# Two attention blocks on one core: loads in one fixed order instead of a simulated queue's order

## Chip, core and metric

The kernel runs on one core of one Trainium2 chip. The metric is the device time of one execution in microseconds (us), median of several. "Span" is the profiled execution from its first to its last instruction, some 2 us less than the device time of that execution. Ratios are the mean time of one kernel's fast runs over the mean of the kernel before's fast runs in the same rounds on the same chip, so they are not quite the ratio of the medians quoted.

## The reference

Twice (A and B, with their own inputs), and concatenated at the end:

```python
B, Sq, D = 16, 64, 640;  H, Sk, Dh = 32, 512, 128          # all bfloat16
q = (x @ wq).reshape(B, Sq, H, Dh).transpose(0, 2, 1, 3)
scores = einsum("bhqd,bhkd->bhqk", q, k_cache) * Dh ** -0.5
p = softmax(scores, axis=-1)
o = einsum("bhqk,bhkd->bhqd", p, v_cache)
out = o.transpose(0, 2, 1, 3).reshape(B, Sq, H * Dh) @ wo
```

The K and V caches are 268 MB of the 292 MB that have to be read.

## The kernel before

The work is cut into 128 *packs*: pack n has four heads of two batches, with two K loads, two V loads (512 KB each), score products, softmax, PV products and a share of the output product. A pack's steps stand at fixed fractions of a "slot" (`AT`), pipelined over some five slots. K has a ring of six packs (`NK`), V of four (`NV`). There are four phases of 32 packs; each has its own wq and wo weights. Loads are listed with a desired time, a time from which their buffer is free, and a rank; a simulated DMA queue puts them in order:

```python
AT = dict(..., KT=(-1.24, -1.0), S=0, ..., PV=1.75, OE=(2.0, 2.06), ..., OP=2.31, ...)
DMA_US = dict(LDK=1.27, LDV=1.29, LDWQ=1.5, LDWO=1.75, LDX=0.45)
# V of pack n (called for n = -2 and -1 too: packs that only fill the pipeline)
op = add("sp", "LDV", (n, b), tv - 0.3, [], [("v", n % cfg.NV, b)])
ready = n - cfg.NV + AT["PV"] + 0.2 if n >= cfg.NV - 2 else -99.0
loads.append((tv - 0.05 if n >= 0 else -99.0, ready, 3, op))
# K of pack n
ready = n - cfg.NK + AT["KT"][b] + 0.25 if n >= cfg.NK else -99.0
loads.append((tk - 0.05, ready, 2, op))
...
add("dve", "VZ", 0, -9.9, [], [("v", i % cfg.NV, b) for i in (-2, -1) for b in range(2)])   # memset of two V slots
add("dve", "BZ", 0, -9.8, ...); add("dve", "WZ", 0, -9.7, ...)                                # two more memsets
...
pending = sorted(loads, key=lambda e: (e[0], e[2])); t_now = -7.0
while pending:
    cand = [e for e in pending[:64] if e[1] <= t_now]        # free buffers first, by desired time
    ...
    progs["sp"].append(e[3])
```

SyncE ("SP") then issues that list in order. Before each load it waits for whoever used the buffer last; the list of such waits comes from the resource names (`("v", slot, b)`). A V load of pack -2 or -1 moves nothing: it is a placeholder that waits like a load and then only raises the semaphore.

```python
if n < 0:
    return None, None            # em_LDV
...
for s, v in waits:
    e.wait_ge(sem[s], v * units(s))
first, last = emitters[kind](e, op)
if last is None:
    e.sem_inc(sem[op.sem], units(op.sem))
    return
```

Of the kernel before, what the change touches and what calls it, by code (L numbers as in the profile page):

```python
# [17 lines left out]
class Cfg:  # L18
# [7 lines left out]
    NR = 2  # L26
    PERIOD = 4
    BASE = 32
    WIDE = (0, 1, 2)
    SLOT_US = 5.6  # L30
    AT = dict(XT=-2.485, XE=-2.28, XC=-0.9, QP=-0.45, QE=-0.24, KT=(-1.24, -1.0), S=0,
              EX=(0.21, 0.32, 0.43, 0.54), RC=(0.53, 0.75), NM=(0.56, 0.69, 0.82, 0.95), TR=1.2,
              TE=(1.26, 1.39), PV=1.75, OE=(2.0, 2.06), ZO=2.11, OP=2.31, OS=2.53, ST=3.374, WP0=-1.75, WP1=-1.6)
    DMA_US = dict(LDK=1.27, LDV=1.29, LDWQ=1.5, LDWO=1.75, LDX=0.45)


class Op:
# [19 lines left out]
def build_plan(dims, cfg, general):  # L57
# [4 lines left out]
    NPH, NBP, NJ = dims["NPH"], dims["NBP"], dims["NJ"]  # L62
    PH = NBP * NJ
    N = NPH * PH
    AT = cfg.AT
    ops = []
    loads = []
    at = {}

    def add(eng, kind, idx, ts, reads=(), writes=()):  # L70
        op = Op(eng, kind, idx, ts, reads, writes)
        ops.append(op)
        at[(kind, idx)] = op
        return op

    def add_output(n):
        g, j = n // NJ, n % NJ
        final = n >= 0 and dims["FINAL"](g // NBP)
        for b in range(2):
            tv = n + AT["PV"]  # L80
            op = add("sp", "LDV", (n, b), tv - 0.3, [], [("v", n % cfg.NV, b)])
            ready = n - cfg.NV + AT["PV"] + 0.2 if n >= cfg.NV - 2 else -99.0
            loads.append((tv - 0.05 if n >= 0 else -99.0, ready, 3, op))
        if n > -2:
            add("pe", "TR", n, n + AT["TR"], [("pn", i) for i in range(4)] + [("ident",)], [("B", 4), ("B", 5)])
        for b in range(2):
            add("dve", "TE", (n, b), n + AT["TE"][b], [], [("B", 4 + b), ("pT", b)])
        add("pe", "PV", n, n + AT["PV"], [("pT", 0), ("pT", 1), ("v", n % cfg.NV, 0), ("v", n % cfg.NV, 1)],
            [("B", 4), ("B", 5), ("B67",)])
        add("act", "OE", (n, 1), n + AT["OE"][0], [], [("B67",), ("oT", 1)])  # L90
        add("act", "OE", (n, 0), n + AT["OE"][1], [], [("B", 4), ("B", 5), ("oT", 0)])
        add("act", "ZO", n, n + AT["ZO"], [("zeros",)], [("B67",)])
        add("pe", "OP", n, n + AT["OP"], [("oT", 0), ("oT", 1), ("wo", j)], [("B67",)])
        if j == NJ - 1:
            bp = g % NBP
            add("dve", "OS", g, n + AT["OS"], [("acc", bp)], [("B67",), ("out_sb",) if final else ("acc", bp)])
            if final:
                add("act", "ST", g, n + AT["ST"], [("out_sb",)], [("out_dram", g)])
# [4 lines left out]
    for g in range(N // NJ + 1):  # L103
        n0 = g * NJ
        txt = n0 + AT["XT"]
        add("pe", "XT", g, txt, [("xn", g % cfg.NXN), ("ident",)], [("SB", 0)])
        if g == N // NJ:
            break
        if dims["FIRST"](g // NBP):
            add("act", "XE", g, n0 + AT["XE"], [], [("SB", 0), ("xs", g % NBP)])  # L110
            op = add("sp", "LDX", g, txt - 0.5, [], [("xn", g % cfg.NXN)])
            loads.append((txt - 2.4, (g - cfg.NXN) * NJ + AT["XT"] if g > cfg.NXN else -7.0, 0, op))
        add("pool", "XC", g, n0 + AT["XC"], [("xs", g % NBP)], [("xT", g % cfg.NX)])
    for ph in range(NPH):
        twp = [ph * PH + j + (AT["WP1"] if ph else AT["WP0"]) for j in range(NJ)]
        for kt in range(dims["KT"] if ph else 0):
            ready = twp[-1] - PH + 0.5 if ph > 1 else NJ - 1 + AT["WP0"] + 0.5
            op = add("sp", "LDWQ", (ph, kt), twp[0] - 0.5, [], [("ws", kt, j) for j in range(NJ)])
            loads.append((ready + 0.5 + 0.5 * kt if ph == 1 else ready + 2.0 + 0.14 * PH * kt, ready, 1, op))
        for j in range(NJ):  # L120
            w = ph * NJ + j
            n0 = ph * PH + j
            add("pool", "WP", w, twp[j], [("ws", kt, j) for kt in range(dims["KT"])], [("wqp", j)])
            if not ph:
                op = add("sp", "LDWQ", (0, j), twp[j] - 0.5, [], [("ws", kt, j) for kt in range(dims["KT"])])
                loads.append((twp[j] - 0.3, -99.0, 1, op))
            tuse = n0 + AT["OE"][0]
            op = add("sp", "LDWO", w, n0 + AT["OP"] - 0.8 * NJ, [], [("wo", j)])
            ready = n0 - NJ + AT["OP"] + 0.2 if ph else -99.0
            loads.append((tuse - 0.3, ready, 4, op))  # L130
    if not general:
        add("pool", "PZ", 0, -9.95, [], [("zeros",)])
    add("dve", "VZ", 0, -9.9, [], [("v", i % cfg.NV, b) for i in (-2, -1) for b in range(2)])
# [3 lines left out]
    for n in range(-2, N):  # L137
        add_output(n)
        if n < 0:
            continue  # L140
        g, j = n // NJ, n % NJ
        add("pe", "QP", n, n + AT["QP"], [("xT", g % cfg.NX), ("wqp", j)], [("SB", 1)])
        add("act", "QE", n, n + AT["QE"], [], [("SB", 1), ("qs", n % cfg.NQ)])
        for b in range(2):
            tk = n + AT["KT"][b]
            add("dve", "KT", (n, b), tk, [("kn", n % cfg.NK, b)], [("kt", n % cfg.NKT, b)])
            op = add("sp", "LDK", (n, b), tk - 0.9, [], [("kn", n % cfg.NK, b)])
            ready = n - cfg.NK + AT["KT"][b] + 0.25 if n >= cfg.NK else -99.0
            loads.append((tk - 0.05, ready, 2, op))
        add("pe", "S", n, n + AT["S"], [("qs", n % cfg.NQ), ("kt", n % cfg.NKT, 0), ("kt", n % cfg.NKT, 1)],  # L150
            [("SB", i) for i in range(4)])
        for i in range(4):
            h = 4 * n + i
            te = n + AT["EX"][i]
            if general:
                add("dve", "MX", h, te - 0.002, [], [("SB", i), ("negmax", h % 4)])
            add("act", "EX", h, te, [("negmax", h % 4)] if general else [],
                [("SB", i), ("p", h % cfg.NP), ("rs", h)])
            add("pool", "NM", h, n + AT["NM"][i], [("p", h % cfg.NP), ("recip", n % cfg.NR, i // 3)], [("pn", i)])
        for a in range(2):  # L160
            add("dve", "RC", (n, a), n + AT["RC"][a], [("rs", 4 * n + i) for i in ((0, 1, 2), (3,))[a]],
                [("recip", n % cfg.NR, a)])
# [3 lines left out]
        add("dve", "FLC", 0, N - 1 + AT["TE"][1] + 0.002, [], [("SB", 0), ("flag",)])  # L166

    progs = {e: sorted((o for o in ops if o.eng == e), key=lambda o: o.ts) for e in ENGINES if e != "sp"}
    progs["sp"] = []
    pending = sorted(loads, key=lambda e: (e[0], e[2]))  # L170
    t_now = -7.0
    while pending:
        cand = [e for e in pending[:64] if e[1] <= t_now]
        if cand:
            e = cand[0]
        else:
            e = min(pending[:64], key=lambda e_: (e_[1], e_[0], e_[2]))
            t_now = float(e[1])
        pending.remove(e)
        progs["sp"].append(e[3])  # L180
        if e[3].kind != "LDV" or e[3].idx[0] >= 0:
            t_now += cfg.DMA_US[e[3].kind] / cfg.SLOT_US

    last_writer = {}
    readers = {}
# [87 lines left out]

    base = {("q_" + eng,): cfg.BASE for eng in ("act", "dve", "pool")}
    counts = dict(base)
# [163 lines left out]
def mha_kernel(nc, blocks, out, cfg=None):  # L439
# [13 lines left out]
    NH = NBLK * NBP * H  # L453
    WIDE = cfg.WIDE

    plans = []
    for general in (False, True):
        dims = dict(NPH=NPH, NBP=NBP, NJ=NJ, KT=KT, FIRST=lambda ph: ph % NSUB == 0,
                    FINAL=lambda ph: ph % NSUB == NSUB - 1)
        plans.append(build_plan(dims, cfg, general))  # L460
    NK, NV, NKT, NX, NXN, NQ, NP, NR = (cfg.NK, cfg.NV, cfg.NKT, cfg.NX, cfg.NXN, cfg.NQ, cfg.NP, cfg.NR)

    with contextlib.ExitStack() as es:
# [101 lines left out]
        def em_LDV(e, op):  # L565
# [5 lines left out]
            dst = v_ring[:, n % NV, b]  # L571
            if j in WIDE:
                ins = e.dma_start(dst.rearrange("p t d -> p (t d)"), src.rearrange("h (p t) d -> (h p) (t d)", t=16))  # L573
# [73 lines left out]
        def exp_views(h):  # L647
            src, dst = ps[:, h % 4, :], p_ring[:, h % NP, :]
            if h // 4 % NJ in WIDE:
                return src, dst  # L650
# [22 lines left out]
        def em_NM(e, op):  # L673
            h = op.idx
            i = h % 4
            if h < 0:
                ins = e.memset(pn_sb[:, :, :].rearrange("p t c -> p (t c)"), 0.0)
                return ins, ins
            if h // 4 % NJ in WIDE:
                dst = pn_sb[:, :, 32 * i:32 * i + 32]  # L680
# [29 lines left out]
        def em_PV(e, op):  # L710
            n = op.idx
            wide = n % NJ in WIDE
            tall, tiles, per = (32, 4, 16) if wide else (64, 2, 8)
# [93 lines left out]
        def run_program(e, eng, p):  # L807
# [7 lines left out]
            for key in sorted(counts):  # L815
                if key[0].startswith("q_"):
                    e.sem_inc(sems[p][key], cfg.BASE)
            for op in prog[:lo]:
# [100 lines left out]
```

## Time and profile before

| | before |
|---|---|
| device time, median of 3 | 766.59 us |
| span of the profiled execution | 764.1 us |
| loaded from HBM | 292.03 MB |
| PE / DVE / ACT / POOL busy | 89 / 69 / 68 / 53 % |
| last V lands | 744.1 us |

The last row is from the trace's landing records: each load raises its semaphore in 16 steps, and the sixteenth is the landing (the two V loads of a pack share a semaphore, so a V landing here is the second one's). PE's busy share counts pipelined products, so by the profile page's own legend it is not the share of its peak. One more view is SyncE's own waits (who waited, for whom; us in all, times, longest us):

```profile
SPq L562 <- PE ps L636: 43.2, 26, 3.3
SPq L573 <- PE ps L721: 24.8, 19, 4.1
...
SPq L800 <- DVE v_ring L525: 4.5, 1, 4.5
```

Line 562 issues K, line 573 V; line 800 is the placeholder's semaphore increment.

### The profile page before, as it was taken

The page shows a single profiled execution, that of the slowest core. Times are in us where ns is not written, and L with a number is a line of the kernel's source. Part 1 is how long each engine was busy: PE and PEld are TensorE (multiplying, and loading weights), DVE is VectorE, ACT ScalarE, POOL GpSimd, SP SyncE. Part 2 cuts the span into 40 slices and gives each one's busy share as a digit, 9 for nine tenths or more (in the row PEclk, how much of TensorE's full clock was granted, in tenths as well). Part 3 has the DMA queues.
Part 4 walks back from the last instruction along what each step waited for, and adds up shares of the span by engine and source line. Part 5 has one row for each costly group of instructions (what it writes and reads, how often), then busy time and mean ns, then how long its engine had stood idle before and what let it go on. Part 6 is the DMA issues. An engine that isn't in the chain of part 4 may idle for free.

```text
span 764.1 us, 57362 instructions
## 1 busy us (share of the span) xinstructions
PE 681.7 (89%) x26518; PEld 527.6 (69%) x26518; DVE 529.5 (69%) x814; ACT 518.8 (68%) x1559; POOL 406.7 (53%) x584
## 2 busy tenths in 40 slices
PE   1659999999999899998988889999999899899995
PEld 1437777777777677776766667777777677777773
DVE  6527777777777767776776677776776576677772
ACT  1437777778777767766766767777766577667773
POOL 4515554554875445554585445555477455454542
PEclk9979999999999999999999999999999999999999
DMA  6999999999999999999999999999999999999960
GB/s 221 390 398 405 408 405 406 405 406 406 407 395 404 407 406 407 407 408 409 406 401 394 405 406 408 405 406 404 406 407 394 397 407 408 407 408 408 406 255 15
DMA packets 99806, 295.15 MB, mean 386 GB/s; under 512 B 9264, under 2 KB 24112, under 8 KB 99760
## 3 DMA queue, kind: packets, MB, share of 16 engines
q1 hardware_dynamic: 97456, 292.06, 97.8%
q10 hardware_dynamic: 2304, 2.62, 1.0%
q14 instruction: 36, 0.29, 0.1%
q8 instruction: 10, 0.16, 0.1%
HBM read 292.03 MB, written 2.62 MB: 386 GB/s over the span
## 4 chain that ended last, share of the span: by engine, by line
SPq 38%; PE 28%; DMA 18%; POOL 6%; issue 5%; DVE 4%; ACT 0%; POOLq 0%; DVEq 0%; ACTq 0%
SPq L562 16%; SPq L573 11%; DMA v_ring<-in_B_v_cache_dram 8%; PE ps L721 7%; SPq L575 6%; PE ps L741 6%; PE ps L636 6%; PE ps L613 5%; POOL pn_sb L686 5%; DMA v_ring<-in_A_v_cache_dram 4%; PE ps L697 4%; DMA kn_ring<-in_A_k_cache_dram 3%; DVE pT_sb L707 2%; SPq L539 2%; DMA kn_ring<-in_B_k_cache_dram 2%
## 5 line engine op out<-in xcount | busy, mean ns | idle before, releaser
L686 POOL TENSOR_SCALAR pn_sb<-p_ring,recip 128x512 bf16<-128x512 bf16 x512 | 344.5, 692 | 330.0 <-DVE recip L670 330.0
L626 DVE STREAM_TRANSPOSE kt_ring<-kn_ring 128x1024 f32<-128x1024 f32 x256 | 307.3, 1225 | 62.2 <-DMA kn_ring<-in_B_k_cache_dram 34.7
L657 ACT ACTIVATE p_ring<-ps 128x512 bf16<-128x512 f32 x512 | 298.3, 598 | 26.4 <-PE ps L636 21.2
L707 DVE COPY pT_sb<-ps 128x1024 bf16<-128x1024 bf16 x258 | 165.3, 682 | 128.9 <-PE ps L697 128.8
L721 PE MATMUL ps<-pT_sb,v_ring 32*128 32x64 bf16 (+1 forms) x14528 | 156.1, 192 | 34.0 <-DMA v_ring<-in_B_v_cache_dram 9.8
L721 PEld LDWEIGHTS ps<-pT_sb,v_ring 32*128 32x128 bf16 (+1 forms) x14528 | 141.7, 92 | 49.1 <-DMA v_ring<-in_B_v_cache_dram 16.2
L741 PE MATMUL ps<-wo_sb,oT_sb 128*128 128x320 bf16 x1040 | 166.0, 303 | 6.0 <-issue 5.0
L613 PE MATMUL ps<-xT_ring,wqp_sb 128*128 128x128 bf16 x2560 | 165.4, 220 | 5.6 <-POOL xT_ring L602 5.6
L729 ACT ACTIVATE oT_sb<-ps 128x256 bf16<-128x256 f32 x260 | 85.6, 381 | 122.5 <-PE ps L721 108.3
L613 PEld LDWEIGHTS ps<-xT_ring,wqp_sb 128*128 128x128 bf16 x2560 | 157.1, 114 | 11.9 <-issue 5.9
L636 PE MATMUL ps<-kt_ring,qs_ring 32*64 32x512 bf16 x4096 | 147.9, 399 | 0.0
L619 ACT ACTIVATE qs_ring<-ps 128x512 bf16<-128x512 f32 x128 | 76.4, 597 | 81.1 <-PE ps L613 80.8
L697 PEld LDWEIGHTS ps<-ident,pn_sb 64*128 64x128 bf16 x4128 | 70.4, 95 | 83.6 <-ACT ps L733 53.5
L741 PEld LDWEIGHTS ps<-wo_sb,oT_sb 128*128 128x128 bf16 x1040 | 91.7, 98 | 43.8 <-issue 5.5
L657 ACT ACTIVATION_READ_ACCUMULATOR p_ring<-ps 128x1 f32 x512 | 106.7, 208 | 0.0
L697 PE MATMUL ps<-ident,pn_sb 64*128 64x64 bf16 x4128 | 84.0, 191 | 23.1 <-POOL pn_sb L686 14.0
L636 PEld LDWEIGHTS ps<-kt_ring,qs_ring 32*64 32x64 bf16 x4096 | 55.9, 104 | 31.7 <-issue 1.4
L670 DVE RECIPROCAL recip<-rowsum 128x3 f32<-128x3 f32 (+1 forms) x256 | 37.6, 161 | 32.2 <-ACT p_ring L657 28.0
L733 ACT ACTIVATE ps<-zeros 128x256 f32<-128x256 bf16 x130 | 51.5, 396 | 0.0
L585 POOL COPY wqp_sb<-ws_sb 128x1280 bf16<-128x1280 bf16 x32 | 39.2, 1254 | 11.9 <-DMA ws_sb<-in_A_wq_dram 11.9
L602 POOL COPY xT_ring<-xs_sb 128x640 bf16<-128x640 bf16 x32 | 22.9, 716 | 3.1 <-PE ps L613 3.1
L592 PE MATMUL ps<-ident,xn_ring 128*128 128x128 bf16 x165 | 14.8, 222 | 8.0 <-DMA xn_ring<-in_A_x_dram 8.0
(25 smaller groups left out, 65.3 us busy)
## 6 DMA issues: line engine op xcount, KB each, us to landing
kn_ring<-in_A_k_cache_dram SPq DMA_DIRECT2D x128, 512.0 KB, 13.7
v_ring<-in_A_v_cache_dram SPq DMA_DIRECT2D x128, 512.0 KB, 13.5
kn_ring<-in_B_k_cache_dram SPq DMA_DIRECT2D x128, 512.0 KB, 14.7
v_ring<-in_B_v_cache_dram SPq DMA_DIRECT2D x128, 512.0 KB, 12.1
wo_sb<-in_A_wo_dram SPq DMA_DIRECT2D x8, 640.0 KB, 13.1
ws_sb<-in_B_wq_dram SPq DMA_DIRECT2D x10, 512.0 KB, 13.5
wo_sb<-in_B_wo_dram SPq DMA_DIRECT2D x8, 640.0 KB, 13.4
ws_sb<-in_A_wq_dram SPq DMA_DIRECT2D x4, 640.0 KB, 9.1
```

The lines of the kernel that those rows point to most:

```text
L562: ins = e.dma_start(kn_ring[:, n % NK, b, :], src)
L573: ins = e.dma_start(dst.rearrange("p t d -> p (t d)"), src.rearrange("h (p t) d -> (h p) (t d)", t=16))
L613: last = e.matmul(ps[:, 1, f * 128:(f + 1) * 128], w[:, kt, f, :], xT_ring[:, xs, kt, :], start=(kt == 0), stop=(kt == KT - 1))
L626: ins = e.transpose(dst, kn_ring[:, n % NK, b, :].bitcast(F32))
L636: last = e.matmul(ps[64 * b:64 * b + 64, i, :], qs_ring[rows, n % NQ, f, b, :], kt_ring[rows, n % NKT, b, :, f // 2, :, f % 2], start=(f = ...
L657: ins = e.activation(dst, src, ACTF.Exp, scale=1.0, accum_out=rowsum[:, h:h + 1])
L686: ins = e.tensor_scalar(dst, src, recip[:, h // 4 % NR, i:i + 1], 1.0, ALU.mult, ALU.mult)
L697: last = e.transpose(pt_bank(b)[:, 64 * c:64 * c + 64], pn_sb[rows, c, :], ident[rows, rows], tile_position=(64 * b, 0))
L707: ins = e.tensor_copy(pT_sb[:, b].rearrange("p t q -> p (t q)"), pt_bank(b))
L721: last = e.matmul(ps[:, 4 + i, 64 * b:64 * b + 64], v_ring[rows, n % NV, b, c, :], pT_sb[rows, b, c, :], start=(t == 0 and i < 2), stop=(t ...
L729: ins = e.activation(oT_sb[:, 2 * a:2 * a + 2, :], o_ps[:, 2 * a:2 * a + 2, :], ACTF.Copy)
L741: last = e.matmul(out_ps[:, s, :], oT_sb[:, i, :], wo_sb[:, 4 * j + i, s * NH0:(s + 1) * NH0], start=(j == 0 and i == 0), stop=(j == NJ - ...
```

## The change

Its intent: drop the simulated queue and give every load a fixed time in slots: V when its slot comes free, K so that it stands beside the V of three packs earlier, x and weights early. The core of the diff:

```diff
+    KLEAD = 2.5
-            op = add("sp", "LDV", (n, b), tv - 0.3, [], [("v", n % cfg.NV, b)])
-            ready = n - cfg.NV + AT["PV"] + 0.2 if n >= cfg.NV - 2 else -99.0
-            loads.append((tv - 0.05 if n >= 0 else -99.0, ready, 3, op))
+            op = add("sp", "LDV", (n, b), tv - 0.3, [], [("v" if n >= 0 else "absent", n % cfg.NV, b)])
+            loads.append((n - cfg.NV + AT["PV"] + 0.2 if n >= 0 else -99.0, 3, op))
 ...
-            ready = n - cfg.NK + AT["KT"][b] + 0.25 if n >= cfg.NK else -99.0
-            loads.append((tk - 0.05, ready, 2, op))
+            loads.append((n - cfg.NV + AT["PV"] + 0.2 - cfg.KLEAD, 2, op))
 ...                                   (x, wq and wo loads: their times alike)
-    pending = sorted(loads, key=lambda e: (e[0], e[2]))
-    t_now = -7.0
-    while pending: ...
+    progs["sp"] = [e[2] for e in sorted(loads, key=lambda e: e[:2])]
```

## The prediction

> **What bounds the kernel now.** I read the page's slices first, then a table by stretches, then the waits of single stretches, then the chain that ended last, and last the trace's landing records.
>
> The page: DMA share by slice, GB/s by slice, and the queue that carries all loads.
>
> ```profile
> DMA  6999999999999999999999999999999999999960
> GB/s 221 390 398 405 408 405 406 405 406 406 407 395 404 407 406 407 407 408 409 406 401 394 405 406 408 405 406 404 406 407 394 397 407 408 407 408 408 406 255 15
> q1 hardware_dynamic: 97456, 292.06, 97.8%
> ```
>
> All slices but the first and the last two move 390 to 409 GB/s. 292.06 MB at 406 GB/s take 719 us of the 764.1 us span: the load stream is nearly the whole kernel. A K or V load is 512 KB, so 0.524 MB / 406 GB/s = 1.29 us; a pack (2 K, 2 V) is 5.2 us. The order of issue sets only *which* load is late, and what is left to do when the last has landed.
>
> Stretches (us, PE, PEld, DVE, ACT, POOL busy, PE clock, DMA share, GB/s):
>
> ```profile
> 100.00:200.00 100.00, 98.38 (x3884) 76.84 (x3883) 75.96 (x119) 77.52 (x233) 54.56 (x81) 1.00 1.03 406
> 600.00:700.00 100.00, 92.78 (x3638) 71.48 (x3634) 71.63 (x109) 68.99 (x210) 50.25 (x75) 0.98 1.03 408
> 735.00:740.00 5.00, 4.96 (x174) 3.77 (x165) 4.22 (x8) 3.66 (x12) 1.91 (x3) 1.00 0.69 248
> 740.00:745.00 5.00, 4.66 (x191) 3.60 (x176) 3.13 (x6) 3.66 (x12) 2.71 (x5) 1.00 0.15 57
> ```
>
> From 60 to 207 us PE is the bound (98% busy; no wait for a load in that stretch) although DMA is saturated too. Later PE is at 91 to 93% and waits for loads, until about 707 us. After 730 us DMA runs out of work and PE is the bound again. The waits between 600 and 710 us that a DMA ended:
>
> ```profile
> PEld ps L721 <- DMA v_ring<-in_B_v_cache_dram: 7.7, 9, 2.0
> PE ps L721 <- DMA v_ring<-in_B_v_cache_dram: 5.0, 6, 1.6
> DVE kt_ring L626 <- DMA kn_ring<-in_B_k_cache_dram: 4.3, 2, 3.8
> ACT oT_sb L729 <- DMA wo_sb<-in_B_wo_dram: 2.1, 1, 2.1
> ```
>
> Late in the kernel it is V that is late, in many small waits (PE pauses before the PV product, L721); K only twice. The chain from its last DMA on:
>
> ```profile
> 691.07 16.75 DMA v_ring<-in_B_v_cache_dram
> 707.81 0.05 issue
> 707.86 1.22 PE ps L721 x128
> 709.07 1.06 PE ps L636 x23
> ```
>
> The PV product at 707.86 us is pack 118's (counted back from pack 127's, at 754.98). From there to the end, 56 us, the chain holds no DMA: PE, POOL and DVE set the pace. That pace, from starts of PV products where nothing is late:
>
> ```profile
> 70.24 1.22 PE L721 MATMUL ps<-pT_sb,v_ring 32*128 32x64 bf16 x128
> ...
> 75.67 1.22 PE L721 MATMUL ps<-pT_sb,v_ring 32*128 32x64 bf16 x128
> ...
> 91.33 1.22 PE L721 MATMUL ps<-pT_sb,v_ring 32*128 32x64 bf16 x128
> ```
>
> 70.24 to 91.33 is four packs: 21.09 us, 5.27 a pack. The stream needs 5.2 plus weights and x. The two are level, which is why a small shift in the order can decide who waits.
>
> **What the Trainium skill says.** "DMA: Bandwidth & Descriptors", section Queues, rings and completion order: each DMA engine consumes a ring's descriptors in ring order. So the order in which SyncE issues is the order in which loads come. The trace agrees: by the landing records, consecutive loads finish about 1.28 us apart in the issued order. The same page, Specifications, gives a fabric ceiling of 435 GB/s; the trace's 406 is below it, and nothing in the change alters sizes or packets, so I expect no other rate. "Trace Analysis", section DMA Instruction — HWDGE: the recorded issue holds neither the semaphore wait nor the data movement, so I take a load's lateness from landings and from the waits of PE and DVE, not from issue durations.
>
> **The change part by part.** Instructions on PE, ACT, DVE and POOL stay the same, in the same order (comparing both built programs); so do the 563 loads and all ring depths. Only SyncE's sequence moves.
>
> 1. *K's lead.* Before, SyncE's order came from a simulated queue, which sent K as far ahead as six K slots allow. The waits of the DMA queue show it: loads of K waited 43.2 us in 26 waits for the score product that frees a K slot. Late in the kernel the order is V118, K123, V119, K124 ...; after, it is V118, K121, V119, K122. So pack 118's V stood before 28 loads (10 K, 18 V) and now stands before 32 (14 K, 18 V). The stream ends at the same moment, so V118 lands 4 x 1.28 = 5.1 us earlier, 702.7 instead of 707.8 us. From 92 to 123 all V move by 0 to 4 loads in this way. That is the gain: V was on the path, K lay ready about 8 us (K121 landed at 699.1).
>
> 2. *What takes V's place.* K121 now lands two loads behind V118, at 705.2 us. DVE transposes it in two halves of 1.23 us, and these stand before the PSUM copies that the next PV needs. Between packs 68 and 91 the kernel before had just this order (V68, K71 ...), and the landing records show K there 1.8 to 2.5 us after the PV product's start at the cost of 0 to 0.6 us a pack. So K costs about 0.5 us of the 5.1: 4.6 left.
>
> 3. *PE's own pace as a cap.* After the last weights (the wo load of pack 99) nothing but K and V comes. PV of pack 101 started at 613.94 us. If nothing were late after it: 24 packs x 5.27 = 126.5 to pack 125 (740.4), plus the 19.0 us that lay between pack 125's PV (745.10) and the end: 759.4, which is 4.7 us less than 764.1. Parts 1 and 3 agree, so about 4.6 us is all there is.
>
> 4. *Weights.* The wo load of a pack now stands after both halves of a K, one load later than before (V97, K100, K100, wo 13). ACT's copy (L729) will wait up to 3 us instead of up to 2.6 at eight places. But the same bytes precede V100 in both orders, and DMA bounds there. 0 to 0.3 us lost, in my estimate. wq of phase 1 is spread among packs 4 to 7 instead of five in a row at 48 us; at that time PE is slowed by pauses labelled "issue", so nothing is gained.
>
> 5. *V issued as soon as its slot is free, K behind it.* SyncE now stops at each V until PV of four packs earlier is done. Nothing runs dry: at 71 us V8 is issued 9.7 us before its first piece lands, with the same loads ahead of it in both orders. While PE is the bound (60 to 207 us) that margin shrinks by 5.27 - 5.19 = 0.08 us a pack, 2 us over 24 packs. 0 us.
>
> Sum: -5.1 + 0.5 + 0.2 = about -4.4 us of 764. The measured time is 766.59, so 762.2.
>
> **Rivals.** *(a) SyncE's stops starve the queue.* For it: each V now waits, and K is stuck behind it with its slot free. Against: the 9.7 us of queue at 71 us, and later landings 13 to 18 us after issue. If it happened from 60 to 207 us, DMA share would fall below 1.0 there, and each percent of 147 us costs 1.5 us; the time would be 766 to 772. *(b) K becomes the bound.* K's lead over V's shrinks from about 8 us early to 2.5 us behind V's landing; if DVE's order makes each late K cost the full 2.5 us, the gain is halved: 764. Against: packs 68 to 91 ran that way. *(c) The end is DMA's anyway.* V127 landed at 744.1, and its PV started 10.9 us later, so that slack takes the whole shift; a gain above 10 us is impossible because the same stream ends at 744.1 in any order without gaps. *(d) The head gains.* V2 and V3 come four loads earlier, wq later; PE started its real pace at 59 us because of pauses that no load ended. DMA's saturation after it swallows it: 0.
>
> **Range and chances.** Centre 762.2: part 3's cap gives 761.9, rival (b) 764, a few pauses more 765. Below 759 a second mechanism would be needed. Range 759.0 to 765.5. Two per cent is 15.3 us: faster by that would need the stream itself to be shorter (2%), slower would need starvation over most of the run (3%).
>
> **What would show it.** Right: DMA share stays 1.03 from 60 to 730 us; the K loads' waits for score products (L562's) vanish and SyncE waits at V; waits of PE at L721 for V after 600 us fall from 12.7 us (both rows) to under 4, waits of DVE for K rise; the last load still lands at 743 to 745 us while PE ends near 759.5; the gap from last landing to the end falls from 20 to about 16 us. Wrong if: DMA share dips in the first 200 us (a), DVE's waits for K reach tens of us late on (b), or the stream ends at another time.

## The result and the profile after

The changed kernel takes 758.43 us (757.98 to 759.13, 4 runs) against 766.69 us (4 runs) in the same rounds: ratio 0.9894, 95% interval 0.9876 to 0.9911. That is 8.1 us by the ratio, nearly twice the 4.4 us predicted, and below the range of 759.0 to 765.5. The span is 756.0 us.

The page's DMA share and GB/s by slice:

```profile
DMA  8999999999999999999999999999999999999980
GB/s 309 394 398 405 406 407 407 405 405 406 403 395 406 406 408 406 407 407 408 408 399 395 406 407 408 405 405 405 406 406 397 394 408 407 407 408 407 406 326 20
```

The middle is as before. The first slice has 309 GB/s instead of 221: at 18.9 us a slice that is 5.8 MB against 4.2 MB, 1.6 MB more, or 4 us of the stream. The load stream *starts earlier*. The head of the timeline says by how much (start us, us, what); before:

```profile
1.71 3.47 DVE L525 MEMSET v_ring<- 128x4096 uint32 x1 [1.71 <-PEq L904]
5.48 0.40 SPq L539 DMA_DIRECT2D xn_ring<-in_A_x_dram  x1
```

and after:

```profile
1.04 0.40 SPq L521 DMA_DIRECT2D xn_ring<-in_A_x_dram  x1
1.49 0.42 SPq L531 DMA_DIRECT2D ws_sb<-in_A_wq_dram  x1
1.71 3.47 DVE L507 MEMSET v_ring<- 128x4096 uint32 x1 [1.71 <-PEq L886]
```

Before, the first load went out 0.30 us after the V ring's memset ended at 5.18 us; after, it goes out at 1.04 us, while that memset has not begun. SyncE's waits after:

```profile
SPq L555 <- PE ps L703: 78.0, 38, 6.0
SPq L557 <- PE ps L703: 26.8, 9, 4.2
```

The 4.5 us row for the memset is gone. So are K's waits; SyncE now stops at V, as intended. The cause is one word of the diff: placeholders now write the resource `"absent"` instead of `"v"`, so they no longer depend on the memset. They stand first in SyncE's list, so before, the whole list stood behind them.

The same stretches as in the prediction (PE, PEld, DVE, ACT, POOL busy, PE clock, DMA share, GB/s), then the waits of 600 to 710 us that a DMA ended, then the last DMA on the chain that ended last:

```profile
100.00:200.00 100.00, 98.37 (x3885) 76.94 (x3885) 76.18 (x120) 77.21 (x232) 55.92 (x83) 1.00 1.03 406
600.00:700.00 100.00, 97.14 (x3779) 75.70 (x3780) 74.07 (x116) 74.08 (x226) 51.75 (x77) 0.98 1.03 407
735.00:740.00 5.00, 4.99 (x220) 4.02 (x220) 1.53 (x4) 3.64 (x12) 2.69 (x4) 1.00 0.18 68
```

```profile
ACT oT_sb L711 <- DMA wo_sb<-in_B_wo_dram: 3.3, 1, 3.3
```

```profile
587.88 12.35 DMA wo_sb<-in_B_wo_dram
600.23 0.02 issue
600.25 0.67 ACT oT_sb L711 x2
```

From 600 to 700 us PE rises from 93 to 97% busy, and no wait for V or K is left; the one DMA wait is ACT's, for the last wo load (wo 15, of pack 99). From 600.2 us to the end the chain holds no DMA. Before, that point was at 707.8 us.

So there are two candidates: the start (4.4 us earlier) and the order late in the kernel. The trace alone doesn't say how they add up. In particular the prediction had argued that an early start is swallowed.

### The profile page after: what moved, and what is told of

Read it like the earlier page. It is cut to its first block, busy times and chain, and to the rows that moved or that the text cites. A ratio compares the mean times of both kernels' runs of the same rounds, so it can differ in the third digit from the quotient of the medians.

```text
span 756.0 us, 57362 instructions
## 1 busy us (share of the span) xinstructions
PE 685.2 (91%) x26518; PEld 530.0 (70%) x26518; DVE 533.2 (71%) x814; ACT 518.5 (69%) x1559; POOL 406.7 (54%) x584
## 4 chain that ended last, share of the span: by engine, by line
PE 40%; SPq 20%; DMA 17%; POOL 9%; DVE 8%; issue 4%; ACT 1%; POOLq 0%; DVEq 0%; ACTq 0%
PE ps L723 10%; PE ps L703 9%; POOL pn_sb L668 9%; PE ps L595 8%; SPq L544 8%; PE ps L618 7%; SPq L555 6%; PE ps L679 6%; DMA kn_ring<-in_B_k_cache_dram 6%; DMA kn_ring<-in_A_k_cache_dram 5%; SPq L557 4%; DMA wo_sb<-in_B_wo_dram 3%; DVE pT_sb L689 3%; DMA v_ring<-in_B_v_cache_dram 2%; DVE kt_ring L608 1%
## 5 line engine op out<-in xcount | busy, mean ns | idle before, releaser
L723 PE MATMUL ps<-wo_sb,oT_sb 128*128 128x320 bf16 x1040 | 169.7, 307 | 6.9 <-issue 5.9
```

Source lines behind the costliest of these rows:

```text
L723: last = e.matmul(out_ps[:, s, :], oT_sb[:, i, :], wo_sb[:, 4 * j + i, s * NH0:(s + 1) * NH0], start=(j == 0 and i == 0), stop=(j == NJ - ...
```

## The experiments

All were timed with five rounds. "x us by the ratio" is (ratio difference) x 766.7.

| run | median us | ratio to before, 95% interval |
|---|---|---|
| changed kernel | 758.43 | 0.9894 (0.9876 to 0.9911) |
| order_only | 763.47 | 0.9947 (0.9932 to 0.9962) |
| start_only | 762.33 | 0.9942 (0.9928 to 0.9957) |
| late_inc | 761.61 | 0.9934 (0.9914 to 0.9954) |
| vz_last | 771.54 | 1.0055 (1.004 to 1.0069) |
| tail_only | 761.91 | 0.9944 (0.9931 to 0.9958) |
| head_only | 766.50 | 0.9999 (0.9986 to 1.0013) |
| lead_4_5 | 764.47 | 0.9976 (0.9962 to 0.999) |
| lead_1_5 | 760.12 | 0.992 (0.9907 to 0.9934) |
| wo_early | 757.63 | 0.9891 (0.9876 to 0.9905) |
| less_wq3 | 752.85 | 0.9831 (0.9818 to 0.9845) |
| less_v | 758.94 | 0.9905 (0.9888 to 0.9921) |
| tail_early | 757.08 | 0.9879 (0.9864 to 0.9895) |

### Which part makes the gain?

*order_only*: the changed kernel with the dependency put back.

```diff
-[("v" if n >= 0 else "absent", n % cfg.NV, b)])
+[("v", n % cfg.NV, b)])
```

> The changed kernel with one part undone: the two placeholder V loads of packs -2 and -1 again wait for DVE's memset of the V ring, so the first load is issued at about 5.5 us instead of 1.0 us. Theory A (the gain has two parts that add: loads start 4.4 us earlier, and the new order of K and V): 762.2 to 762.9 us, that is the changed kernel's 758.4 plus 3.8 to 4.5, and the last V lands at 744 us as in the kernel before. Rival B (the early start is swallowed because DMA is saturated afterwards anyway, and the order is worth the whole 8 us): 758.4 to 759. Rival C (the start alone makes the gain, the order is worth nothing): 766.7.

*start_only*: the kernel before with `"absent"` alone (the same line, the other way).

> The kernel before with that one part alone: the placeholders no longer wait for the memset; order of loads as before. Theory A: 762.3 to 763.0 us, the last V lands 3.7 to 4.4 us earlier than 744.1, waits for V late in the kernel as in the kernel before. Rival B: 766.7. Rival C: 758.4.

The order alone is worth 0.0053, 4.1 us; the start alone 0.0058, 4.4 us. Together 8.5, measured 8.1: they add. Theories B and C fall. In the profiled runs start_only's first load goes out at 1.04 us and its last V lands at 739.8 us (before: 744.1), and its waits for V between 600 and 710 us are 7.5 us (PEld) and 3.8 us (PE), before 7.7 and 5.0: the whole stream has moved 4.3 us, and V is about as late within it as before.

### Is it really the wait at the head of SyncE's list?

*late_inc* keeps the dependency and moves only the placeholders' place in the list of the kernel before:

```diff
+    absent = [o for o in progs["sp"] if o.kind == "LDV" and o.idx[0] < 0]
+    progs["sp"] = [o for o in progs["sp"] if o not in absent]
+    progs["sp"][8:8] = absent
```

> The kernel before; the wait for the memset is kept, but the placeholders stand after the first eight loads in SyncE's order instead of ahead of the first. If what costs is that the wait stands at the head of SyncE's line (theory A): as start_only within 0.5 us, first issue at about 1.0 us. If the missing dependency itself did something else: 766.7.

It gives 0.9934, within its interval the same as start_only; its first load goes out at 0.79 us. So the dependency did no harm there; its place at the head of the list cost the time.

*vz_last* makes the wait longer without adding work: the memset comes third on DVE instead of first.

```diff
-    add("dve", "VZ", 0, -9.9, ...)
+    add("dve", "VZ", 0, -9.6, ...)
```

> The kernel before with DVE's three memsets in another order: the V ring's comes last, so it ends about 4.4 us later (1.76 us for the PSUM memset and 2.19 us for the wo memset go ahead of it, with gaps), and nothing is added. Theory A: the first load is issued at about 9.9 us and the end moves by the same: 770.6 to 771.4 us. Rival B (saturation swallows the start): 766.7 to 767.5.

Its head (start us, us, what):

```profile
3.58 2.19 DVE L533 MEMSET wo_sb<- 128x2560 uint32 x1 [0.52 <-issue]
6.57 3.47 DVE L525 MEMSET v_ring<- 128x4096 uint32 x1 [0.80 <-issue]
10.34 0.40 SPq L539 DMA_DIRECT2D xn_ring<-in_A_x_dram  x1
```

The first load goes out 4.9 us later than before (10.34 against 5.48) and the kernel takes 0.0055, 4.2 us longer. From 1.0 to 5.5 to 10.3 us of first issue the time goes up by 4.4 and 4.2 us: almost one for one.

### Where does the order pay?

*tail_only* is the kernel before (its early wait kept) with its own order up to the V of pack 100 and the changed kernel's order from there; *head_only* is the mirror. `fixed` holds the changed kernel's times.

```diff
+    cut = fixed[id(at[("LDV", (100, 1))])]
+    key = lambda o: fixed[id(o)]
+    progs["sp"] = ([o for o in progs["sp"] if key(o) <= cut]
+                   + sorted((o for o in progs["sp"] if key(o) > cut), key=key))
```

> The kernel before (wait for the memset kept): its own order up to the V of pack 100, and from there on the changed kernel's order. Theory A2 (the order pays only through V of the last quarter; earlier order is swallowed because the same bytes have to come): 761.5 to 763 us, as order_only (763.5) or up to 1.5 us less, since the wo loads of packs 96 to 99 keep their old place. Rival (the whole order has to change): 766 to 767.

> The mirror of tail_only: the changed kernel's order up to the V of pack 100, then the order of the kernel before; the wait for the memset kept. If the order pays only after pack 100: 766 to 767.5, as the kernel before. If the earlier order pays too: 764 to 765.

tail_only has the whole of it (0.0056, 4.3 us), head_only nothing (0.0001). Both predicted values were met. Up to pack 100 another order of the same bytes changed nothing; after it, 28 packs of order were worth 4 us.

The trace of tail_only shows something that the changed kernel hides. Between 600 and 710 us:

```profile
DVE kt_ring L638 <- DMA kn_ring<-in_B_k_cache_dram: 15.6, 25, 3.9
```

In the changed kernel no such row is left there. In tail_only the wo loads keep their old, earlier places. Pack 101's PV product starts at 613.8 us (in order_only at 615.7), and the K loads land 1.3 to 2.1 us after the start of the PV product of three packs earlier; in the changed kernel it is 0.3 us before to 0.6 us after (packs 100 to 124, every third one read). The last DMA on the chain of tail_only is a K load that landed at 732 us. So which load is the last to be needed differs between these two kernels, though their order after pack 100 is the same.

### How much lead of K is right?

*lead_4_5* and *lead_1_5* are the changed kernel with another lead from pack 9 on:

```diff
-            loads.append((n - cfg.NV + AT["PV"] + 0.2 - cfg.KLEAD, 2, op))
+            loads.append((n - cfg.NV + AT["PV"] + 0.2 - (4.5 if n > 8 else cfg.KLEAD), 2, op))
```

> The changed kernel with K's lead at 4.5 packs instead of 2.5 from pack 9 on (K of pack n+5 behind V of pack n, as the kernel before has it near its end). Theory A2: every late V stands behind four more loads, 5.1 us; in the changed kernel V lay ready 2.0 to 2.8 us before its product from pack 104 on, so 2.3 to 4 us are lost: 760.7 to 762.5, and PE waits for V again after 600 us. Rival (K's lead is not what pays, the fixed order is): 758.4.

> The changed kernel with K's lead at 1.5 packs from pack 9 on: K of pack n+2 behind V of pack n, so K comes two loads (2.56 us) later against its use. In the changed kernel K lands between 0.7 us before and 0.6 us after the PV product's start from pack 100 on, and up to 2 us after it cost nothing. So DVE's waits for K rise and the time with them, by 0.5 to 2 us: 759 to 760.5. If K has more room than I think: 758.4 or less.

lead_4_5 loses 0.0082, 6.3 us: more than expected, and not as expected. PE waits for no V after 600 us. The last DMA on its chain is wo 15:

```profile
594.11 12.11 DMA wo_sb<-in_B_wo_dram
```

It landed at 606.2 us, where the changed kernel's landed at 600.2. Four more K loads (5.1 us) stand ahead of it, and they pass to the end in full; I had reckoned with a V that had 2 to 2.8 us to spare. The other 0.9 us of the 6.0 I have not traced.

lead_1_5 loses 0.0026, 2.0 us, at the upper end of what was expected (the two intervals just overlap), and the expected wait is in its trace. Between 600 and 710 us, and the last DMA on its chain up to 710 us:

```profile
DVE kt_ring L608 <- DMA kn_ring<-in_B_k_cache_dram: 15.4, 24, 3.8
```

```profile
694.13 14.05 DMA kn_ring<-in_B_k_cache_dram
```

In the changed kernel neither is there in that stretch: K two loads later has to be waited for by DVE. The sum of the row does not measure the loss, though: tail_early below has a like one (16.9 us in 25 waits, 580 to 710 us) and is not slower than the changed kernel. So 2.5 lies between a lead that delays what else is needed and one that delays K itself.

### What bounds the changed kernel?

*wo_early* puts each wo load ahead of the two K loads before it (`AT["OP"] + 0.2` becomes `AT["OP"] + 0.1`).

> The changed kernel with the wo load of a pack issued right behind V of the same j, ahead of the two K loads behind which it stands now. In the changed kernel the last load on the chain is wo 15 (ACT waits 3.3 us for it, 6.9 us in three waits between 580 and 620 us) and from there the chain holds no load. Two loads less ahead of it are 2.56 us, K of packs 99 to 102 come 1.6 us later. Theory (wo bounds, then PE's pace to the end): 1 to 2.5 us less, 756 to 757.4. If K takes wo's place: 758 to 759.

It gains 0.0003: a miss. Between 580 and 620 us its waits are

```profile
DVE kt_ring L608 <- DMA kn_ring<-in_B_k_cache_dram: 10.4, 4, 3.8
PEld ps L703 <- DMA v_ring<-in_B_v_cache_dram: 5.4, 3, 2.0
ACT oT_sb L711 <- DMA wo_sb<-in_B_wo_dram: 5.2, 2, 3.0
```

In the changed kernel they were 1.7 us for K, none for V and 6.9 us for wo. A K load took wo's place: the last DMA on the chain of wo_early is a K that landed at 600.4 us, where wo 15 of the changed kernel landed at 600.2. At pack 100 the kernel has asked for everything loaded so far. Two runs that are wrong test that.

*less_wq3* takes bytes away *before* pack 100 (packs 69 to 90), *less_v* takes three times as many away *after* it:

```diff
-                ins = e.dma_start(ws_sb[:, i].rearrange("p j c -> p (j c)"), src[:, i, c:c + NJ * 512])
+                few = 1 if ph == 3 else NJ
+                ins = e.dma_start(ws_sb[:, i, 0:few].rearrange("p j c -> p (j c)"), src[:, i, c:c + few * 512])
```

```diff
-            if j in WIDE:
+            if n >= 108 and b == 1 and j in WIDE:
+                ins = e.dma_start(dst[:, 0:4, :].rearrange("p t d -> p (t d)"),
+                                  src.rearrange("h (p t) d -> (h p) (t d)", t=16)[:, 0:4 * DH])
+            elif j in WIDE:
```

> The changed kernel, made wrong on purpose: the five wq loads of the last phase (issued between packs 69 and 90) bring a quarter of their bytes, 1.97 MB less in all, 4.8 us at 406 GB/s. If the load stream bounds up to pack 100 (theory): 4 to 5 us less, 753.4 to 754.4. If PE or something else bounds there: under 1 us less.

> The changed kernel, made wrong on purpose: 15 V loads of packs 108 to 126 bring a quarter of their bytes, 5.9 MB less in all, 14.5 us at 406 GB/s. If from pack 101 on PE's own pace sets the end (theory): 0 to 1 us less, 757.4 to 758.4. If the load stream still bounds at the end: 5 us less or more.

1.97 MB less before pack 100: 0.0063, 4.8 us less than the changed kernel, the size of its 4.8 us of stream. 5.9 MB less after pack 100: no gain (0.9905 against 0.9894, intervals overlap), although the last V now landed at 733.7 instead of 740.5 us. So the changed kernel is one piece after the other: the load stream sets the time up to pack 100, PE's pace from there. less_v takes bytes only from pack 108 on; for packs 101 to 107 the evidence is the chain, which holds no DMA after 600.2 us. (less_wq3 passed the comparison with the reference although it used stale wq columns. The reference's inputs explain that, as an estimate from reference.py: q is about 0.01 and K 0.1 in size, so the scores are about 0.001 and the softmax is almost even, whatever wq is.)

### A version that beats both?

*tail_early* joins the best parts: order of the kernel before up to pack 100, the changed one after it, no wait for the memset.

> tail_only with the early start: the order of the kernel before up to pack 100 (wo loads one or two loads earlier than in the changed kernel), the changed kernel's order after it, and no wait for the memset. The two parts add: 761.9 - 4.4 = 757.5; it beats the changed kernel only if the wo waits (3.3 us at wo 15) cost it something: 756.5 to 758.

757.08 us, 0.9879: clearly better than the kernel before. Against the changed kernel (0.9894) the intervals overlap; 1 us may be there, the runs don't settle it.

## Why the prediction was wrong, point by point

- **The step that failed** is the premise under the change part by part, "Only SyncE's sequence moves", with part 1's "The stream ends at the same moment", rival (c)'s "the same stream ends at 744.1 in any order without gaps", and rival (d)'s "DMA's saturation after it swallows it: 0". The change also took away a wait: 4.4 us (start_only). The stream begins 4.4 us earlier, and its last V landed at 740.5 us, not 744.1. The 0.9 us that this lacks of 4.4 goes with the new order: the last V of start_only landed the full 4.3 us earlier, that of order_only 1.4 us later than before (745.4 us). The 4.5 us row stood in SyncE's waits of the kernel before and the word `"absent"` in the diff. I read both and joined neither to the other.
- Rival (d) had the logic upside down. If a saturated stream bounds the time, *order* at its head is swallowed (head_only: nothing), but its *start* is not: every later byte moves with it (start_only, late_inc, vz_last).
- **Part 1, K's lead:** right in size. The order alone gave 4.1 us where the sum said 4.4, all of it after pack 100 (tail_only). V118 landed at 703.5 us in order_only, where the prediction had 702.7, and at 707.8 before.
- **Part 2, K takes V's place at 0.5 us:** not in the changed kernel, which after 600 us waits for no K at all, it seems because wo had held PE back (part 4). It is there in tail_only and tail_early, where K comes late: from pack 101's PV product to the end they took 145.7 and 145.4 us against 145.0 in the changed kernel, so 0.4 to 0.7 us (single profiled runs), the predicted size. The landings read for it from packs 68 to 91 run from 1.2 to 3.1 us after the PV product's start, not 1.8 to 2.5.
- **Part 3, PE's pace as a cap:** right. Its sum leaves 145.5 us from pack 101's PV product to the end; the changed kernel took 145.0, the kernel before 150.2. So in these profiled runs 5.1 us of the gain came after that product, and the other 3.0 before it: it started at 610.96 instead of 613.94 us, roughly the 4.4 us of the start less what wo took.
- **Part 4, wo at 0 to 0.3 us:** too small in the profiled runs. ACT waited 10.0 us for wo between 580 and 620 us in order_only, against 5.4 before, and pack 101's PV started at 615.7 instead of 613.9 us: 1.8 us. The count of loads, "one load later than before", was wrong: by the order of issue, the wo load of pack 97 keeps its place, that of 98 comes one load later and that of 99 (wo 15) two, about 2.6 us; wo 15 landed at 605.1 us in order_only and 601.6 before. In the timed runs the loss is not shown: tail_only, with wo in its old places, is by ratio only 0.0003, 0.2 us, better than order_only. There K is late instead, as under part 2.
- **Part 5 and rival (a), starvation:** right to leave at 0. DMA share stays 1.03 from 60 to 700 us. (The 5.19 us a pack in its sum is in no trace; nothing hangs on it. Nor did V2 and V3 in rival (d) come four loads earlier, but six and five.)
- Of what was to be seen: K's waits on SyncE gone (yes), V's waits after 600 us under 4 us (0), waits of DVE for K up (no: 4.3 to 0 after 600 us; over the whole run 61.1 to 66.4), last landing unmoved (no: 3.5 us earlier), last landing to end 16 us (15.4).

A second PE loss hides in wo's wait. "TensorE: Matmul & The Clock Gate" in the Trainium skill, Part 1: The HAM clock gate, says that PE's clock falls to half after an idle window of about 3.4 us. Here a pause of 2.50 us before 600.96 us was followed by a stretch at a mean granted clock of 0.72 (600 to 606 us), 0.50 from 600.5 to 603.9: its output product took 2.21 us instead of 1.26. So a wait can cost PE more than its length.

```profile
600.96 1.03 PE L679 MATMUL ps<-ident,pn_sb 64*128 64x64 bf16 x32 [2.50 <-ACT oT_sb L711]
601.93 2.21 PE L723 MATMUL ps<-wo_sb,oT_sb 128*128 128x320 bf16 x8
```

This doesn't explain the result: the kernel before has such a stretch too (0.50 from 607.8 to 611.2 us, after a pause of 1.9 us), and so has order_only (0.50 from 607.2 to 610.6).

## What to carry to other kernels

When one stream of loads bounds a kernel, look at the moment of its first issue before anything else: here each microsecond of wait at the head of the issuing engine's list was nearly a microsecond of the whole, and a placeholder carried it. Order inside the stream paid only near its end, where it decides which loads still stand ahead of what is needed last; a test that takes bytes away on each side of the suspected hand-over finds that point. A renamed resource in a dependency table is a removed wait: compare the waits of both built programs, not only their instructions.

## What the Trainium skill lacked or had wrong

- "DMA: Bandwidth & Descriptors", Latency and other measured facts, speaks of two slower DMA engines and calls the suspected cause specific to GpSimd's path. Here all loads were issued from SyncE, and still the 16 completions of one load drifted apart over the kernel before: 0.9 us from first to last for the first K load, 7.2 us for the second K load of pack 121. The records don't tell which engine is late; the last one sets every landing.
- The same page and "Perfetto Trace Analysis", section DMA Instruction — HWDGE, give no figure for what an issue costs once many loads are in flight. Here the issue of a K load took 0.33 us at least, 0.8 to 1.1 us in the median and 5.6 us at most.
- "TensorE: Matmul & The Clock Gate" puts the threshold at an idle window of about 3.4 us; in the changed kernel the half clock came after pauses of 2.50 us and even 1.76 us (before 586.5 us), while one of 2.02 us (before 417.1 us) left the clock full.
- None of the pages that I read has that the start of a bounding load stream passes on one for one: 4.4 us earlier gave 4.4 us, 4.9 us later gave 4.2 us.
